# Loads of a decode layer spread over two DMA queues, in whole loads, with a smaller wq side load

## Chip, cores, metric

One core of one Trainium2 chip runs the whole program. The metric is the device time of one execution in microseconds (us), as the median of several executions; lower is better. "PE" is TensorE (PEld its weight loads), "DVE" is VectorE, "ACT" is ScalarE, "SP" is the engine that issues the DMAs of the sync queue. "SPq" and "ACTq" are DMA issues by those two.

## The reference, cut to what matters

One decoding step, batch 4, one token each: layer norm, attention with 32 query heads over the last 2048 positions of a cache with 4 KV heads, output projection, layer norm, SwiGLU. All tensors are bfloat16.

```python
q  = layernorm(x) @ wq                         # x 4x1024, wq 1024x4096
p  = softmax(q . k * 128**-0.5)                # k, v: 4 x 4 heads x 2048 x 128 are read
h  = x + (p @ v) @ wo                          # wo 4096x1024
hn = layernorm(h)
out = h + (silu(hn @ w1) * (hn @ w3)) @ w2     # w1, w3 1024x3584, w2 3584x1024
```

There are 55.6 MB to read and only four rows to work on, so the time is that of reading.

## The kernel before

All loads go through one 160 KiB wide ring of SBUF and one queue. A list gives their order; `load_next()` issues the next one at fixed places in the program. A load waits on SP until its place in the ring is free.

```python
def load_rows(at, src, n, r0, m):
    t = ring[:, at : at + m * n]
    nc.sync.dma_start(out=t, in_=src[:, r0 * n : (r0 + m) * n])
    ...
def load_kv(at, src, b):                 # two batches, two DMAs of 2 MB
    for k in range(BS): ... nc.sync.dma_start(...)

CE = 512
SETS = [(0, 5, 4), (80, 3, 2), (104, 3, 2)]      # first row, engines, column blocks
def load_side(r0, ne, ns): ...           # the last CE columns of the last wq row of 128
                                         # partitions, loaded into few partitions instead
def load_tail(at, src, n, r0, m): ...    # the second half of wq without those columns
plan = [
    ("wq", load_rows, (0, wq_v, N_Q, 0, 4)),
    ("side", load_side, SETS[0]), ("side", load_side, SETS[1]), ("side", load_side, SETS[2]),
    ("wq", load_tail, (32 * KIB, wq_v, N_Q, 4, 4)),
    ("k", load_kv, (64 * KIB, A_k_cache, 0)), ("k", load_kv, (96 * KIB, A_k_cache, 2)),
    ("v", load_kv, (128 * KIB, A_v_cache, 0)), ("v", load_kv, (0, A_v_cache, 2)),
    ("wo", load_rows, (32 * KIB, wo_v, D, 0, 32)),
    ("w1", load_rows, (96 * KIB, w1_v, N_F, 0, 8)),
    ("w3", ... two halves), ("w2", ... 17, 7, 3 and 1 rows),
]
```

The side loads are a tuned detail. A normal load uses 16 DMA engines, each with 8 of the 128 partitions. A side load uses only 5 or 3 of them. So 512 columns (1024 bytes) of one row of each partition are taken from all 16 engines (8 KB each) and given to five: 32 rows to three engines, 16 rows to two.

The K part transposes each tile on PE and copies it out of PSUM in turn on DVE and ACT:

```python
for u, (b, n) in enumerate(units):          # 16 units
    for t in range(NJ // TB):               # two tiles each
        ... 8 transposes on PE ...
        if nt % 2 == 0: nc.vector.tensor_copy(...)
        else:           nc.scalar.copy(...)
```

## Time and profile before

| | before |
|---|---|
| median (range) of runs at the time of the prediction | 138.0 us (137.88 to 138.04) |
| read from HBM | 55.59 MB |
| first byte to last landing | 1.7 to 132.8 us |
| rate in that stretch | 426 GB/s, DMA share 1.00 |
| last landing to end of the span | 3.4 us |

The first fence holds lines of the page of the kernel before: busy times by engine, then the span in 40 slices (busy share of the DMA engines in tenths, and GB/s), then the DMA queues with packets, MB and the share of the time of 16 engines.

```profile
PE 73.8 (54%) x1050; PEld 45.0 (33%) x1050; DVE 43.4 (32%) x79; ACT 31.1 (23%) x36; POOL 1.7 (1%) x8
...
DMA  5999999999999999999979999989899999989970
GB/s 156 463 464 404 404 438 405 424 428 438 433 428 419 429 443 428 429 522 477 462 327 443 481 409 404 477 371 477 354 430 426 438 455 442 430 389 419 421 288 5
...
q1 hardware_dynamic: 2731, 55.58, 95.6%
q8 instruction: 8, 0.13, 0.3%
q10 hardware_dynamic: 48, 0.02, 0.1%
q14 instruction: 2, 0.02, 0.0%
```

Queue q1 is the sync queue; it carries nearly everything (q10, ACT's, has 0.02 MB) and is never without work.

The next fence is the stretch table over 1.6 to 132.3 us (stretch and its length, busy time of PE, PEld, DVE, ACT, POOL with counts, PE clock, DMA share, GB/s).

```profile
1.60:132.30 130.70, 73.10 (x1039) 44.68 (x1043) 42.76 (x77) 30.72 (x35) 0.67 (x3) 0.79 1.00 426
```

A share of 1.00 says that the 16 engines were busy for the whole stretch. Then the timeline at the end (start us, busy us, engine, line, operation, in brackets the idle time before it and what ended it). `hgT` are the activations that w2 is multiplied with, `y_ps` the sum:

```profile
120.18 1.70 DVE L477 STREAM_TRANSPOSE hgT<-hg 128x896 bf16<-128x896 bf16 x1
...
126.09 3.82 PE L485 MATMUL y_ps<-ring,hgT 128*32 128x256 bf16 x68 [7.08 <-DMA ring<-in_B_w_dram]
...
130.34 1.22 PE L485 MATMUL y_ps<-ring,hgT 128*32 128x256 bf16 x28 [0.43 <-DMA ring<-in_B_w_dram]
...
132.18 0.92 PE L485 MATMUL y_ps<-ring,hgT 128*32 128x256 bf16 x16 [0.63 <-DMA ring<-in_B_w_dram]
...
133.15 0.37 ACT L495 CAST res<-y_ps 128x256 bf16<-128x256 f32 x1 [26.41 <-PE y_ps L485]
```

PE waits for w2's data at every step, so the end of the kernel is the last landing plus a fixed tail.

### The profile page before, as it was taken

Reading aid. Unit: us, or ns where it says so; the run is one execution under the profiler, and the core shown is the slowest. Engines: PE = TensorE matmul, PEld = TensorE weight load, DVE = VectorE, ACT = ScalarE, POOL = GpSimd, SP = SyncE. Lnnn points to the kernel's source line nnn. Section 1 sums busy time; section 2 is a strip of 40 time slices with the busy share of each in tenths; the row PEclk is TensorE's granted clock in tenths of the full one; section 3 lists DMA queues with packets and bytes.
Section 4 is the critical chain, followed back from the end, with each engine's and each line's share of the span. In section 5 each row is a group of like instructions: output and inputs, shape, how many; then the busy total and the mean of one; then the engine's idle time right before and its main releaser. Section 6 shows DMA issues by size and latency. Waiting matters only on the chain.

```text
span 136.1 us, 2343 instructions
## 1 busy us (share of the span) xinstructions
PE 73.8 (54%) x1050; PEld 45.0 (33%) x1050; DVE 43.4 (32%) x79; ACT 31.1 (23%) x36; POOL 1.7 (1%) x8
## 2 busy tenths in 40 slices
PE   0202980979898989810535906793096440900960
PEld 0200220267474747400024905571043210300840
DVE  6820000044243434471984001206100695080000
ACT  3000000016555555518385200000002300000001
POOL 5000000000000000000000000000000000000000
PEclk9999999999999999997555555579757777555577
DMA  5999999999999999999979999989899999989970
GB/s 156 463 464 404 404 438 405 424 428 438 433 428 419 429 443 428 429 522 477 462 327 443 481 409 404 477 371 477 354 430 426 438 455 442 430 389 419 421 288 5
DMA packets 2789, 55.75 MB, mean 410 GB/s; under 512 B 311, under 2 KB 471, under 8 KB 731
## 3 DMA queue, kind: packets, MB, share of 16 engines
q1 hardware_dynamic: 2731, 55.58, 95.6%
q8 instruction: 8, 0.13, 0.3%
q10 hardware_dynamic: 48, 0.02, 0.1%
q14 instruction: 2, 0.02, 0.0%
HBM read 55.59 MB, written 0.01 MB: 408 GB/s over the span
## 4 chain that ended last, share of the span: by engine, by line
DMA 54%; PE 24%; ACT 11%; DVE 5%; SPq 2%; issue 1%; ACTq 0%
DMA ring<-in_B_w_dram 40%; DMA ring<-in_A_wq_dram 15%; PE kt_ps L315 10%; ACT kT L321 5%; PE scores_ps L300 5%; ACT z L356 3%; PE q_ps L259 3%; SPq L119 2%; PE g_ps L455 2%; DVE rmax L332 2%; ACT Pm L337 2%; PE OT_ps L378 2%; DVE pT L346 1%; DVE z L352 1%; ACT L337 1%
## 5 line engine op out<-in xcount | busy, mean ns | idle before, releaser
L321 ACT COPY kT<-kt_ps 128x1024 bf16<-128x1024 bf16 x16 | 15.9, 1013 | 13.1 <-PE kt_ps L315 13.1
L315 PE MATMUL kt_ps<-ident,ring 128*128 128x128 bf16 x256 | 17.8, 230 | 0.0
L315 PEld LDWEIGHTS <-ring 128*128 128x128 bf16 x256 | 15.8, 104 | 4.9 <-issue 4.9
L319 DVE COPY kT<-kt_ps 128x1024 bf16<-128x1024 bf16 x16 | 11.1, 692 | 16.2 <-PE kt_ps L315 16.2
L259 PE MATMUL q_ps<-ring,xnT 128*4 128x512 bf16 x63 | 7.2, 626 | 10.5 <-DMA ring<-in_A_wq_dram 10.5
L378 PE MATMUL OT_ps<-z,ring 128*128 128x32 bf16 x256 | 7.5, 188 | 9.0 <-ACT z L356 5.0
L455 PEld LDWEIGHTS <-hnT 128*32 128x32 bf16 x128 | 5.3, 137 | 19.3 <-issue 16.6
L300 PE MATMUL scores_ps<-kT,qz 128*32 128x512 bf16 x64 | 9.9, 610 | 2.9 <-ACT kT L321 2.9
L455 PE MATMUL u_ps<-ring,hnT 128*32 128x448 bf16 x64 | 6.4, 576 | 8.2 <-DMA ring<-in_B_w_dram 8.2
L378 PEld LDWEIGHTS <-ring 128*128 128x128 bf16 x256 | 7.4, 105 | 9.8 <-issue 9.7
L485 PE MATMUL y_ps<-ring,hgT 128*32 128x256 bf16 x112 | 5.8, 375 | 8.3 <-DMA ring<-in_B_w_dram 8.1
L455 PE MATMUL g_ps<-ring,hnT 128*32 128x448 bf16 x64 | 5.5, 529 | 5.2 <-DMA ring<-in_B_w_dram 5.2
L485 PEld LDWEIGHTS <-hgT 128*32 128x32 bf16 x112 | 4.5, 130 | 10.2 <-issue 5.9
L259 PEld LDWEIGHTS <-xnT 128*4 128x4 bf16 x63 | 2.0, 115 | 14.8 <-issue 14.7
L277 DVE TENSOR_SCALAR q_sb<-q_ps 128x512 bf16<-128x512 f32 x1 | 0.7, 692 | 19.5 <-PE q_ps L259 19.5
L495 ACT CAST res<-y_ps 128x256 bf16<-128x256 f32 x1 | 0.4, 372 | 26.4 <-PE y_ps L485 26.4
L356 ACT ACTIVATE z<-pt_ps,mask 128x512 bf16<-128x512 f32 x8 | 5.3, 687 | 3.5 <-DVE z L352 3.5
L348 PE MATMUL pt_ps<-pT,perm 128*128 128x512 bf16 x4 | 2.4, 608 | 6.8 <-DVE pT L346 6.8
L278 ACT ACTIVATE q_sb<-q_ps 128x512 bf16<-128x512 f32 x1 | 0.6, 597 | 23.6 <-DVE q_sb L277 23.6
L405 PE MATMUL y_ps<-ring,o 128*32 128x256 bf16 x128 | 5.5, 352 | 0.8 <-DVE o L394 0.8
L352 DVE TENSOR_SCALAR z<-pt_ps,mask 128x512 bf16<-128x512 f32 x8 | 5.5, 738 | 1.2 <-ACT z L356 0.8
L469 DVE RECIPROCAL eg<-eg 128x896 f32<-128x896 f32 x1 | 5.8, 5754 | 0.0
(79 smaller groups left out, 50.2 us busy)
## 6 DMA issues: line engine op xcount, KB each, us to landing
ring<-in_A_k_cache_dram SPq DMA_DIRECT2D x4, 2048.0 KB, 25.4
ring<-in_A_v_cache_dram SPq DMA_DIRECT2D x4, 2048.0 KB, 39.0
ring<-in_B_w_dram SPq DMA_DIRECT2D x1, 7168.0 KB
ring<-in_B_w_dram SPq DMA_DIRECT2D x2, 3584.0 KB, 23.3
ring<-in_B_w_dram SPq DMA_DIRECT2D x1, 4352.0 KB
ring<-in_A_wq_dram SPq DMA_DIRECT2D x1, 4096.0 KB, 12.1
ring<-in_A_wq_dram SPq DMA_DIRECT2D x1, 3968.0 KB, 19.8
ring<-in_B_w_dram SPq DMA_DIRECT2D x1, 1792.0 KB
```

The costliest lines, as they stand in the source:

```text
L259: nc.tensor.matmul(q_ps[QD * g : QD * g + B, hf * 512 : hf * 512 + n], lhsT=xnT[:, kc, :], rhs=wq_t[:, c0 : c0 + n], start=(kc == 0), stop ...
L300: nc.tensor.matmul(scores_ps[QD * g : QD * (g + 1), n * 512 : (n + 1) * 512], lhsT=qz_v[:, z0 : z0 + QD], rhs=kT_v[:, g, :, :], start=(b = ...
L315: nc.tensor.transpose(out=kt_ps[:, jj, :], in_=k_v[:, n * NJ + t * TB + jj, :], identity=ident[:])
L319: nc.vector.tensor_copy(out=kT[:, t * TB : (t + 1) * TB, :], in_=kt_ps[:])
L321: nc.scalar.copy(out=kT[:, t * TB : (t + 1) * TB, :], in_=kt_ps[:])
L352: nc.vector.tensor_scalar(out=z[:, :, g, :], in0=pt_ps[:], scalar1=mask[:, g : g + 1], scalar2=None, op0=ALU.mult)
L356: nc.scalar.mul(out=z[:, :, g, :], in_=pt_ps[:], mul=mask[:, g : g + 1])
L378: nc.tensor.matmul(OT_ps[:, b, :], lhsT=loaded["v"][b][:, j, :], rhs=PTz[j // NJ][:, (j % NJ) * B + b, :, :], start=(j == 0), stop=(j == J ...
L405: nc.tensor.matmul(y_ps[QD * j : QD * (j + 1), :], lhsT=o4[:, i, :, :].rearrange("p b s -> p (b s)"), rhs=loaded["wo"][i][:, j * CG : (j + ...
L455: nc.tensor.matmul(out_ps[QD * j : QD * (j + 1), hf, :HF], lhsT=hnT[:, k, :], rhs=loaded[kind][k][:, c0 : c0 + HF], start=(k == 0), stop=( ...
L469: nc.vector.reciprocal(out=eg[:], in_=eg[:])
L485: nc.tensor.matmul(y2_ps[QD * j : QD * (j + 1), :], lhsT=hgT[:, i, :], rhs=loaded["w2"][i][:, j * CG : (j + 1) * CG], start=False, stop=(i ...
```

## The change

Its intent: spread whole loads over the sync queue and ACT's queue, so that two loads are in flight, and move fewer wq columns with fewer side loads. The number of bytes stays the same. The core of the diff:

```diff
-    BS = 2
-        nc.sync.dma_start(out=t, in_=...)                 # load_rows
+    def load_rows(at, src, n, r0, m, q=nc.sync):
+        tc.keep_in_program_order(q.dma_start(out=t, in_=...))
+    def load_kv(at, src, b, q=nc.sync):                   # one batch, one DMA
-    CE = 512
-    SETS = [(0, 5, 4), (80, 3, 2), (104, 3, 2)]
+    CE = 352
+    SETS = [(0, 5, 4), (80, 3, 4)]
+    Q2 = nc.scalar
         ("k", load_kv, (96 * KIB, A_k_cache, 2)),
+        ("k", load_kv, (112 * KIB, A_k_cache, 3, Q2)),
         ("v", load_kv, (128 * KIB, A_v_cache, 0)),
+        ("v", load_kv, (144 * KIB, A_v_cache, 1, Q2)),
         ("v", load_kv, (0, A_v_cache, 2)),
+        ("v", load_kv, (16 * KIB, A_v_cache, 3, Q2)),
-        ("w1", load_rows, (96 * KIB, w1_v, N_F, 0, 8)),
+        ("w1", load_rows, (96 * KIB, w1_v, N_F, 0, 4)),
+        ("w1", load_rows, (124 * KIB, w1_v, N_F, 4, 4, Q2)),
-        ("w3", load_rows, (28 * KIB, w3_v, N_F, 4, 4)),
+        ("w3", load_rows, (28 * KIB, w3_v, N_F, 4, 4, Q2)),
...
+        load_next({1: 2, 4: 2, 7: 2}.get(u, 0))           # in the K loop
```

More of the change, by code (lines that the diff above doesn't have):

```diff
@@ L88 @@
     ring = stream.tile([P, RING], BF16)
-    def load_rows(at, src, n, r0, m):
+    def load_rows(at, src, n, r0, m, q=nc.sync):
         t = ring[:, at : at + m * n]
-        nc.sync.dma_start(out=t, in_=src[:, r0 * n : (r0 + m) * n])
+        tc.keep_in_program_order(q.dma_start(out=t, in_=src[:, r0 * n : (r0 + m) * n]))
         return [t[:, k * n : (k + 1) * n] for k in range(m)]
-    def load_kv(at, src, b):
-        out = []
-        for k in range(BS):
-            v = ring[:, at + k * JK * Dh : at + (k + 1) * JK * Dh]
-            nc.sync.dma_start(
-                out=v,
-                in_=src[b + k, :, Sk - W : Sk, :].rearrange("g (pp j) d -> pp g (j d)", pp=PK),
-            )
-            out.append(v.rearrange("p (j d) -> p j d", d=Dh))
-        return out
+    def load_kv(at, src, b, q=nc.sync):
+        v = ring[:, at : at + JK * Dh]
+        rows = src[b, :, Sk - W : Sk, :].rearrange("g (pp j) d -> pp g (j d)", pp=PK)
+        tc.keep_in_program_order(q.dma_start(out=v, in_=rows))
+        return [v.rearrange("p (j d) -> p j d", d=Dh)]
     N_Q, N_F = Hq * Dh, F
-    CE = 512
-    SETS = [(0, 5, 4), (80, 3, 2), (104, 3, 2)]
+    CE = 352
+    SETS = [(0, 5, 4), (80, 3, 4)]
     def load_side(r0, ne, ns):
@@ L131 @@
         ("side", load_side, SETS[1]),
-        ("side", load_side, SETS[2]),
         ("wq", load_tail, (32 * KIB, wq_v, N_Q, 4, 4)),
         ("k", load_kv, (64 * KIB, A_k_cache, 0)),
+        ("k", load_kv, (80 * KIB, A_k_cache, 1)),
         ("k", load_kv, (96 * KIB, A_k_cache, 2)),
+        ("k", load_kv, (112 * KIB, A_k_cache, 3, Q2)),
         ("v", load_kv, (128 * KIB, A_v_cache, 0)),
+        ("v", load_kv, (144 * KIB, A_v_cache, 1, Q2)),
         ("v", load_kv, (0, A_v_cache, 2)),
+        ("v", load_kv, (16 * KIB, A_v_cache, 3, Q2)),
         ("wo", load_rows, (32 * KIB, wo_v, D, 0, 32)),
-        ("w1", load_rows, (96 * KIB, w1_v, N_F, 0, 8)),
+        ("w1", load_rows, (96 * KIB, w1_v, N_F, 0, 4)),
+        ("w1", load_rows, (124 * KIB, w1_v, N_F, 4, 4, Q2)),
         ("w3", load_rows, (0, w3_v, N_F, 0, 4)),
-        ("w3", load_rows, (28 * KIB, w3_v, N_F, 4, 4)),
+        ("w3", load_rows, (28 * KIB, w3_v, N_F, 4, 4, Q2)),
         ("w2", load_rows, (56 * KIB, w2_v, D, 0, 17)),
@@ L158 @@
     nc.scalar.dma_start(out=x_sb[:], in_=x_flat)
-    load_next(8)
+    load_next(7)
     ident = const.tile([P, P], BF16)
@@ L263 @@
                     start=(kc == 0),
-                    stop=(kc == KC - 1 or (kc == KC - 2 and c0 + 512 == N_Q)),
+                    stop=(kc == KC - 1),
+                    skip_group_check=(c0 + 512 == N_Q),
                 )
         if kc == RQ - 1:
-            load_next()
             for k, np_ in enumerate(sl):
@@ L274 @@
                     stop=False,
+                    skip_group_check=True,
                 )
@@ L325 @@
             emit_scores(u - 1)
-        if u == NSB * BS - 1:
-            load_next()
+        load_next({1: 2, 4: 2, 7: 2}.get(u, 0))
     emit_scores(len(units) - 1)
+    load_next()
     rmax = act.tile([P, 1], FP32)
@@ L384 @@
             )
-        if b % BS == BS - 1:
+        if b % 2 == 1:
             load_next()
```

## The prediction

> **What bounds the kernel now.** The 16 DMA engines. The DMA view gives 55.6 MB read. The stretch table over 1.6 to 132.3 us shows a DMA share of 1.00 and 426 GB/s. The Trainium skill, page "DMA: Bandwidth & Descriptors", section Specifications, names a fabric ceiling of 435 GB/s; the trace agrees (packets of 28 to 64 KB move at 27.0 to 27.1 GB/s per engine, 16 KB packets at 26.8). So there is no idle time to fill: what is idle is 1.7 us before the first byte and 3.4 us after the last load (matmuls, cast, store). PE is busy 54%. By the chain of waits PE ends last because w2 lands last, at 132.8 us.
>
> The records of packets and landings show engine skew: per load, 11 engines land about 1.5 us before the slowest after wq; at the end 5 are early (131.0 to 131.6 us) and 11 late (132.4 to 132.8). Eight instruction fetches of 16 KB each cost one engine about 1.4 us (0.94 for the fetch, 0.5 more for the packet it overlaps). Side loads cost their engines a comparable amount; the late group is both kinds together.
>
> **What the change does.**
> 1. Two queues. The same skill page ("Issuing engines are not separate DMA queues") says both run on the same 16 engines and interleave. Bytes stay the same, and the single queue never ran dry: w1 was issued at 76.0 us, wo landed at 80.1 to 82.1. Only the few ns per packet can shrink. Estimate: K/V loads follow each other in 4.83 to 4.90 us against 4.82 at the ceiling; over the whole kernel at most 0.5 us.
> 2. Order. From K batch 3 on two loads share the engines, so each lands later. k2 lands near 43 us instead of 38.2, when its transposes start. w1's first half may land near 101 instead of 98.9, w3's first half near 116 with its second half earlier. Then 64 instead of 32 w3 matmuls (2 x 3.2 us) follow 116 us: hgT is ready near 125.3 instead of 121.9, still before w2 lands (126.1). Slack falls from 4.1 to under 1 us.
> 3. ACT issues five loads, about 0.6 us each (its issues now: 0.58 to 0.66). The three in the K phase may lengthen it by 0.5 to 2 us; loads are queued ahead of it.
> 4. CE 352. Each engine that carries no side load moves 2.5 KB more: 0.1 us later at the end. One side issue fewer (0.87 us on SP) and shorter side matmuls are hidden behind wq's loads.
>
> **On the critical path:** up to -0.5 us (packets), +0.1 us (balance), 0 to +0.5 us (w2 starting late, more delayed instruction fetches).
>
> **Predicted:** 137.8 us, 137.0 to 138.8 in 8 of 10. Faster by over 2%: 0.03; within 2%: 0.94; slower: 0.03.
>
> **Signs.** Right: bytes unchanged, 426 to 429 GB/s from first byte to last, last landing within 1 us of 132.8, a second queue carrying about 13 to 14 MB, w1 and w3 halves landing close together, K phase ending later without a later finish. Wrong step 2: PE idle before w2's first matmul ended by DVE, not DMA.
>
> **What would make it wrong.** Two active queues raising or lowering an engine's rate; instruction fetches waiting behind two large packets and stalling PE at the tail; fetches falling on other engines, so that the last engine ends more than 0.5 us earlier or later; ACT blocked by a load's wait while a copy is due.

## The result

The changed kernel took 138.48 us in the median of four runs (138.25 to 138.55), the kernel before 138.02 us (137.88 to 138.08). The ratio is 1.0032, with a 95% interval from 1.0014 to 1.0049. A ratio here is the mean time of one kernel's fast runs over that of the other's of the same rounds, so not quite the ratio of the medians. The change costs 0.3%: small, within 2% as forecast, but clear of noise and of the opposite sign to the forecast 137.8.

The same lines of the page of the changed kernel:

```profile
PE 73.1 (53%) x1051; PEld 45.0 (33%) x1051; DVE 43.1 (32%) x77; ACT 31.4 (23%) x36; POOL 1.7 (1%) x8
...
DMA  5999999999999999999999989999999999999960
GB/s 156 461 462 424 404 394 433 432 417 441 436 417 441 408 441 436 499 405 465 403 489 432 408 362 453 433 428 410 428 445 436 424 420 432 479 408 388 413 251 2
...
q1 hardware_dynamic: 2152, 41.94, 71.9%
q10 hardware_dynamic: 768, 13.66, 23.4%
q8 instruction: 8, 0.13, 0.3%
q14 instruction: 2, 0.02, 0.0%
```

ACT's queue (q10) now carries 13.66 MB, a quarter. The stretch table of the changed kernel:

```profile
1.60:132.30 130.70, 72.25 (x1035) 44.64 (x1036) 42.54 (x75) 31.01 (x35) 0.67 (x3) 0.78 1.00 426
```

The share and the rate are what they were. Two queues neither filled anything nor slowed the 16 engines together. The end of the timeline of the changed kernel:

```profile
122.89 1.70 DVE L476 STREAM_TRANSPOSE hgT<-hg 128x896 bf16<-128x896 bf16 x1
...
126.59 3.82 PE L484 MATMUL y_ps<-ring,hgT 128*32 128x256 bf16 x68 [4.88 <-DMA ring<-in_B_w_dram]
...
130.84 1.01 PE L484 MATMUL y_ps<-ring,hgT 128*32 128x256 bf16 x28 [0.42 <-DMA ring<-in_B_w_dram]
...
132.65 0.94 PE L484 MATMUL y_ps<-ring,hgT 128*32 128x256 bf16 x16 [0.81 <-DMA ring<-in_B_w_dram]
...
133.64 0.37 ACT L494 CAST res<-y_ps 128x256 bf16<-128x256 f32 x1 [24.06 <-PE y_ps L484]
```

The activations are ready 2.7 us later than before (the transpose starts at 122.89, not 120.18), yet PE's wait still ends with the DMA. So the reordered loads ate slack only. What moved is the moment at which each part of w2 is complete and PE goes on: 126.59 instead of 126.09, 130.84 instead of 130.34, and the cast at the end 133.64 instead of 133.15. These are the 0.5 us of the two profiled runs (138.55 and 138.01).

### Which engine was last

In these traces a load over all 16 engines leaves 16 landing records, one for each engine, and PE goes on after the last of them. Here are the 16 landing times of the last w2 load, sorted, from the trace's landing records:

```
before: 130.97 131.09 131.30 131.64 132.40 132.41 132.41 132.45 132.58 132.59 132.61 132.62 132.68 132.69 132.76 132.77
after:  131.03 131.21 131.35 131.56 132.43 132.44 132.51 132.64 132.65 132.66 132.76 132.78 132.79 132.87 132.91 133.26
```

Fifteen engines are about where they were, at most 0.19 us later. One is 0.35 us behind all the others, and the kernel waits for it. (The prediction speaks of 5 early engines and 11 late ones; for this load the list of the kernel before has 4 and 12.)

The packet records have no engine number. But an engine starts each packet 3 to 4 ns before the recorded end of the packet before it, and all the engines go through the same known list of loads. With these two rules the records fall into 16 chains. The bytes of each chain confirm the split: each engine without side rows has 3.468 MB in the changed kernel, plus 16 KB exactly where a fetch of q8 is in its chain. This is a reconstruction of mine. Its table, one line per engine (end of its last w2 packet, side rows that it carries, instruction fetches on it):

```
before                                    after
130.68   0 rows                           130.69   0 rows
130.73   0 rows                           130.92   0 rows
131.01   0 rows                           131.06   0 rows
131.32  16 rows                           131.25  16 rows
132.07   0 rows  16 KB at  86.1           132.11  32 rows
132.10   0 rows  16 KB at 104.1           132.16  32 rows
132.13  32 rows                           132.18   0 rows  16 KB at  86.2
132.13   0 rows  16 KB at  42.9           132.22   0 rows  16 KB at 130.9
132.27   0 rows  16 KB at  92.6           132.29   0 rows  16 KB at  93.7
132.30  32 rows                           132.34   0 rows  16 KB at 106.5
132.31   0 rows  16 KB at  54.6           132.35  16 rows   8 KB at  60.6
132.32   0 rows  16 KB at  31.5           132.49   0 rows  16 KB at  54.1
132.34   0 rows  16 KB at 130.4           132.50   0 rows  16 KB at  80.1
132.37  32 rows                           132.52   0 rows  16 KB at  42.0
132.41   0 rows  16 KB at  80.1           132.61   0 rows  16 KB at  27.5
132.46  16 rows   8 KB at  60.2           132.93  32 rows   8 KB at  93.9
```

The kernel before is in balance. Eight engines are hit by a 16 KB fetch, each by one, and each is held up by 1.40 to 1.42 us: about 0.9 us for the fetch and 0.5 us more for the packet that follows (after the fetch at 130.4, spread over the next four packets, which are of 2 KB). None of the eight has side rows. The engines with 32 rows end together with them, and so does the one with 16 rows and an 8 KB fetch (0.84 us). The changed kernel has an 8 KB fetch that the kernel before hasn't: at 93.9 us, on an engine with 32 rows, 0.78 us. That engine is the last one.

The DMA view of 65 to 134 us shows the extra packet. Kernel before:

```profile
q1 hardware_dynamic: 1120, 28.31, 95.4%
q8 instruction: 5, 0.08, 0.4%
```

Changed kernel:

```profile
q1 hardware_dynamic: 963, 20.12, 67.8%
q10 hardware_dynamic: 362, 8.29, 28.1%
q8 instruction: 5, 0.08, 0.4%
q14 instruction: 1, 0.01, 0.0%
```

Both pages count two q14 packets. In the kernel before they come at 60.2 and 135.6 us, the second after the last load; in the changed kernel at 60.6 and 93.9 us.

Whose instructions are they? In all the traces with such a second packet, it starts when ACT has begun 63 to 69 of the instructions that the trace has (64 in the kernel before at 135.6 us, 64 in the changed kernel at 93.9 us). The first q14 packet, at 55.3 to 60.6 us in all twelve traces, does not follow ACT: ACT has then begun anything from 21 to 57 instructions, DVE 59 to 67. Where ten copies move from ACT to DVE (e6 and e10 below) it comes at 56.3 and 55.3 us instead of 60.6; where copies are added to ACT (e7, e8) it stays near 60, at 59.0 and 60.5. The q8 packets go with PE: in the kernel before the first four come after 241, 505, 771 and 1217 of its instructions (weight loads counted), and the fourth comes after 1217 in eleven of the twelve kernels, whose ACT streams run from 53 to 90 instructions in the trace. Their spacing is not even, though. So the second q14 packet is read here as an instruction fetch of ACT, the first as one of DVE, and q8 as PE's. The Trainium skill agrees in part: "Runtime: NRT & Kernel Launch", section Terms, says that the engines' instruction memory is refilled in 16 KiB blocks (the q8 packets are 16 KB, these two q14 packets 8 KB), and "CRC Debugging", section Comparing the Two Runs, puts the sequencers' refill DMAs on queue 14 (here on q8 too).

So the theory (A): the five loads on ACT's queue are five more instructions, with their waits eight more, in ACT's stream. ACT reaches its next block before the last load instead of after it, the fetch goes through one of the 16 busy engines, and it meets one of the three that carry most side rows. The smaller CE adds a little on all the engines without side rows.

Rivals: (B) two queues at once cost every engine something; (D) the smaller CE is the cause, as the balance is off. A fourth, that w2 waits for the activations, falls with the timeline above.

### The profile page after: what moved, and what is told of

Its sections match the earlier page's. It is cut to its first block, busy times and chain, and to the rows that moved or that the text cites. A ratio compares the mean times of both kernels' runs of the same rounds, so it can differ in the third digit from the quotient of the medians.

```text
span 136.7 us, 2344 instructions
## 1 busy us (share of the span) xinstructions
PE 73.1 (53%) x1051; PEld 45.0 (33%) x1051; DVE 43.1 (32%) x77; ACT 31.4 (23%) x36; POOL 1.7 (1%) x8
## 3 DMA queue, kind: packets, MB, share of 16 engines
q10 hardware_dynamic: 768, 13.66, 23.4%
HBM read 55.59 MB, written 0.01 MB: 407 GB/s over the span
## 4 chain that ended last, share of the span: by engine, by line
DMA 82%; PE 12%; SPq 2%; ACT 1%; DVE 1%; issue 0%; ACTq 0%
DMA ring<-in_B_w_dram 56%; DMA ring<-in_A_wq_dram 15%; DMA ring<-in_A_k_cache_dram 11%; PE kt_ps L315 5%; PE q_ps L258 3%; PE g_ps L454 2%; PE scores_ps L300 2%; SPq L113 1%; PE qt_ps L281 1%; ACT kT L321 1%; DVE q_sb L277 1%; SPq L92 0%; ACT res L494 0%; PE y_ps L484 0%; ACTq L321 0%
## 5 line engine op out<-in xcount | busy, mean ns | idle before, releaser
L315 PE MATMUL kt_ps<-ident,ring 128*128 128x128 bf16 x256 | 19.1, 230 | 1.2 <-DVE kT L319 0.7
L454 PE MATMUL u_ps<-ring,hnT 128*32 128x448 bf16 x64 | 5.4, 519 | 9.1 <-DMA ring<-in_B_w_dram 9.1
L454 PE MATMUL g_ps<-ring,hnT 128*32 128x448 bf16 x64 | 6.1, 577 | 7.2 <-DMA ring<-in_B_w_dram 7.2
```

The lines of the kernel that those rows point to most:

```text
L315: nc.tensor.transpose(out=kt_ps[:, jj, :], in_=k_v[:, n * NJ + t * TB + jj, :], identity=ident[:])
L454: nc.tensor.matmul(out_ps[QD * j : QD * (j + 1), hf, :HF], lhsT=hnT[:, k, :], rhs=loaded[kind][k][:, c0 : c0 + HF], start=(k == 0), stop=( ...
```

## The experiments

Ten kernels, five rounds each; all gave correct results. "Cost" is what the second q14 packet (ACT's fetch) delayed its engine in the profiled run, from the reconstruction; the next columns give the end of the latest engine and the time of the same run.

| run | median us | ratio to before (95%) | ACT fetch (2nd q14) at, on rows | cost us | latest engine | profiled run us |
|---|---|---|---|---|---|---|
| before | 138.02 | | 135.6, after the loads | | 132.46 | 138.01 |
| after | 138.48 | 1.0032 (1.0014 to 1.0049) | 93.9, 32 rows | 0.78 | 132.93 | 138.55 |
| e1_queues_only | 138.61 | 1.0049 (1.0036 to 1.0061) | 94.0, 32 rows | 0.67 | 132.89 | 138.50 |
| e2_cols_only | 138.04 | 1.0005 (0.9992 to 1.0018) | 136.0, after the loads | | 132.68 | 138.18 |
| e3_one_queue | 138.00 | 0.9998 (0.9984 to 1.0011) | 135.9, after the loads | | 132.49 | 138.01 |
| e4_w_on_act | 138.08 | 1.0006 (0.9993 to 1.0018) | 111.9, 32 rows | 0.55 | 132.66 | 138.22 |
| e5_kv_on_act | 138.39 | 1.0028 (1.0015 to 1.0041) | 104.5, 32 rows | 0.66 | 132.85 | 138.37 |
| e6_two_queues_no_fetch | 138.13 | 1.0011 (0.9999 to 1.0023) | none | | 132.57 | 138.15 |
| e7_one_queue_fetch | 138.12 | 1.0013 (1.0001 to 1.0025) | 71.6, 32 rows | 0.55 | 132.76 | 138.28 |
| e8_fetch_earlier | 138.09 | 1.0009 (0.9996 to 1.0022) | 71.3, 32 rows | 0.55 | 132.58 | 138.12 |
| e9_even_side | 138.36 | 1.0031 (1.0018 to 1.0043) | 93.6, 28 rows | 0.62 | 132.93 | 138.53 |
| e10_queues_no_fetch | 138.20 | 1.0014 (1.0001 to 1.0028) | none | | 132.53 | 138.20 |

In all twelve profiled runs the time less the end of the latest engine is 5.50 to 5.67 us. The latest engine decides the time.

### Taking the change apart

**e1_queues_only**: the changed kernel with the side loads as before (cut: a third side load in the list and the lines that go with it).

```diff
-    CE = 352
-    SETS = [(0, 5, 4), (80, 3, 4)]
+    CE = 512
+    SETS = [(0, 5, 4), (80, 3, 2), (104, 3, 2)]
```

> The changed kernel with 512 wq columns moved in three side loads, as before; the queues and the order stay changed. Before 138.0, after 138.5 us. Theory A (the last of 16 engines sets the end; the 0.5 us is 0.1 us of extra wq bytes on the engines without side loads plus 0.35 us of one straggler engine that is hit by one more instruction fetch, the 8 KB one near 94 us): 138.3 to 138.4, the last landing near 133.1 us, one landing some 0.35 us behind the others. Theory B (switching between two queues costs every engine): 138.4 to 138.5, all engines later by about the same. Theory D (the wq share alone is the cause): 138.0.

It came out at 138.61, worse than the changed kernel. (D) falls: without the smaller CE the loss is not less. In the profiled run the engine with 32 rows and the fetch at 94.0 us ends at 132.89, next after it 132.45. The expectation of 138.3 to 138.4 missed: it took 0.1 us off for CE, though a larger CE gives the loaded engines more, and the straggler is one of those.

**e2_cols_only**: the kernel before with `CE = 352` and two side loads.

> The kernel before with 352 wq columns moved in two side loads, one queue as before. Theory A: 138.1 us, plus 0.1 us on the unsided engines, last landing near 132.9, no straggler, no 8 KB instruction fetch near 94 us. Theory B: 138.0. Theory D: 138.4 to 138.5.

138.04: the columns alone cost nothing that can be told from zero. The 0.1 us that was expected lies inside the interval.

**e3_one_queue**: the changed kernel with `Q2 = nc.sync`.

> The changed kernel with every load on the sync queue: same loads, same sizes, same 352 columns. Theory A: 138.1 us, since ACT has five instructions' worth of issues fewer and its fetch near 94 us goes away; last landing near 132.9, no straggler. Theory B: 138.0 to 138.1. Theory D: 138.5.

138.00: cutting the loads differently, another order and CE 352 cost nothing on one queue. So the loss needs ACT's issues. (A) and (B) are still both possible.

**e4_w_on_act** and **e5_kv_on_act** split ACT's five loads. In e4 `Q2` is taken from K batch 3 and V 1, 3; in e5 from the halves of w1 and w3.

> The changed kernel with only the two weight halves (w1, w3) on ScalarE's queue; K batch 3 and V 1, 3 go to the sync queue. Theory A: what counts is where the 8 KB instruction fetch of ACT falls; with two issues instead of five it should come later than 94 us or after the last load, then 138.1 us, otherwise a straggler and 138.4 to 138.5. Theory B: two queues are active for 36 of the some 65 us that they were, so about half the loss: 138.25.

> The changed kernel with only K batch 3 and V 1, 3 on ScalarE's queue; the halves of w1 and w3 go to the sync queue. Counting the instructions of ACT in the traces so far, its second 8 KB instruction fetch comes with its 64th instruction; here that falls between 94 and 112 us. Theory A (one more fetch in front of the last load, on an engine that is already late): between 138.1 and 138.5, with an engine some 0.3 us behind the rest in the last landing if it is over 138.3. Theory B (two queues at once cost every engine, in the K and V stage): 138.4 to 138.5.

e4 lost nothing clear (1.0006), e5 nearly all (1.0028). Under (A) alone that is a surprise for e4, as its fetch comes before the last load and on an engine with 32 rows. The reconstruction shows the size: 0.55 us in e4, 0.66 in e5. From 0.55 us the straggler of e4 is 0.20 us behind the next engine in the profiled run, which was its slowest run (138.22; the others 138.00 to 138.16). Under (B) e4 and e5 should have shared the loss, unless only the K and V stage costs, as (B) is put for e5: 138.39 is at the edge of what it asked for there. These two runs do not decide that; e6, e8 and e10 do.

### Taking the fetch away, or adding it

**e6_two_queues_no_fetch**: the changed kernel, with ten ACT copies less. DVE has time for them.

```diff
-            if nt % 2 == 0:
+            if nt % 2 == 0 or u >= 6:
                 nc.vector.tensor_copy(...)
```

> The changed kernel whole, both queues as in it, but the K copies of units 6 to 15 all go to VectorE, so that ScalarE has 10 instructions fewer and its 64th comes after the last load. Theory A: no 8 KB instruction fetch between 65 and 133 us, no straggler, last landing near 132.9, 138.0 to 138.15 us. Theory B: 138.4 to 138.5, as the queues are used alike.

138.13, where (B) asked for 138.4 to 138.5. The DMA view of 65 to 134 us of this kernel has no q14 line, with the queues used as in the changed kernel:

```profile
q1 hardware_dynamic: 968, 20.45, 68.9%
q10 hardware_dynamic: 331, 7.78, 26.3%
q8 instruction: 5, 0.08, 0.4%
```

No engine with side rows stands behind the rest: the three with 32 rows end by 132.11, the latest of all, with a fetch of PE, at 132.57.

**e10_queues_no_fetch**: the same edit on e1, the worst kernel.

> The queues-only kernel (512 columns in three side loads as before, 138.61) with the K copies of units 6 to 15 on VectorE, so that ACT's 64th instruction and its fetch come after the last load. Account: two queues cost nothing by themselves, so as before, 137.9 to 138.1. Rival (the two queues themselves): 138.5 to 138.65.

138.20 instead of 138.61, so most of the loss is gone with the fetch; but it isn't quite the 137.9 to 138.1 that was expected. Some 0.1% (0.01 to 0.28) is left. The edit also moves copies to DVE, so neither run isolates the fetch perfectly. The intervals of e1 (from 1.0036) and e10 (to 1.0028) do not meet; those of the changed kernel and e6 overlap a little, but no run of e6 (137.98 to 138.19) is as slow as the fastest of the changed kernel (138.25).

**e7_one_queue_fetch**: the kernel before, with ten one-element copies on ACT before the q phase.

```diff
+    dum = const.tile([P, 16], FP32)
+    for i in range(10):
+        nc.scalar.copy(out=dum[:1, i : i + 1], in_=eps_t[:1, :])
```

> The kernel before with 10 one-element copies on ScalarE in its idle time before the q phase, so that its 64th instruction comes near 94 us; one queue. Theory A: 138.2 to 138.4, with one engine some 0.3 us behind in the last landing (138.0 to 138.1 if the fetch meets an early engine). Theory B: 138.0, as one queue is used.

138.12, ratio 1.0013, just clear of 1. The fetch came at 71.6 us, not near 94. It met an engine with 32 rows, which ended at 132.76, 0.28 us behind the next. So the straggler can be made on one queue, with no change to a load. Its cost of 0.55 us is the small one again, and so is the loss. (B) expected 138.0.

**e8_fetch_earlier**: the changed kernel, with 14 such copies, so that the fetch moves.

> The changed kernel with 14 such copies, so that the fetch moves some 20 to 30 us earlier. Theory A: as the engines have no idle time, a fetch costs the same whenever it comes before the last load: 138.2 to 138.6, unless it meets an early engine. Theory B: 138.5.

138.09. This misses (A) as it was put: the fetch at 71.3 us is on an engine with 32 rows, and yet the time is nearly that of the kernel before. The reconstruction shows a cost of 0.55 us instead of 0.78; that engine ends at 132.48, below the latest at 132.58. (B) falls here: both queues are used as in the changed kernel, and most of the loss is gone (all five runs, 138.00 to 138.17, are below the changed kernel's fastest, though the intervals overlap a little).

So a fetch doesn't cost the same whenever it comes. At 71 us and at 112 us it cost 0.55 us, between 93 and 105 us 0.62 to 0.78. With an engine that is otherwise level with the rest, this is the difference between 0.1% and 0.3 to 0.5%. Why the cost differs isn't settled. In the changed kernel, e5 and e9 a 16 KB fetch of PE was in flight at the same time or had ended less than 0.3 us before it; in e1 it had ended 0.6 us earlier; in the three cheap ones the nearest was over 4 us away. That is a coincidence in seven runs, not a test, and it does not carry over to the first q14 packet: that one cost 0.83 to 0.84 us in all twelve runs, in nine of them with the nearest fetch of PE over 4 us away.

### Moving the side rows

**e9_even_side**: the changed kernel, the same columns spread evenly (cut as in e1).

```diff
-    SETS = [(0, 5, 4), (80, 3, 4)]
+    SETS = [(0, 5, 4), (80, 5, 2), (120, 2, 1)]
```

> The changed kernel with the same 352 columns spread evenly: 24 rows on each of five engines (four more on two of them) instead of 32 on three and 16 on two. ACT's fetch near 94 us has landed on a fully loaded engine in every trace, the one near 60 us on a half loaded one. Account (sum of side rows and fetches on one engine): the engine with the second fetch carries 4 to 8 rows fewer, so it ends 0.15 to 0.3 us earlier, the one with the first fetch as much later; 138.2 to 138.35 against 138.48 of the changed kernel. Rival (the two queues themselves, or the fetch wherever it falls): 138.4 to 138.6.

138.36, no gain, but the engines did as the account says. The one with the second fetch and now 28 rows ended at 132.46 instead of 132.93, among the rest. The one with the first q14 fetch (60.6 us; the expectation takes it for ACT's) rose from 16 to 24 rows and from 132.35 to 132.93, and was now the straggler, 0.41 us behind the next. The forecast for the total was 138.2 to 138.35: the first fetch (0.83 us) is the dearer of the two, and that was not weighed. It suggests why the tuned side loads are uneven: with the uneven ones, the first q14 fetch is on an engine with the lesser side load in every trace.

No version beat the kernel before. There is little left to win: three engines without rows and fetches end some 1.5 us early, but the side loads cannot reach them, as all the side rows went to the same five engines.

## Why the prediction was right or wrong

- **Class, range: right.** 138.48 lies within 137.0 to 138.8, and "within 2%" held. The core of the argument held too: 55.59 MB, DMA share 1.00 and 426 GB/s in both kernels. It agrees with the Trainium skill, "DMA: Bandwidth & Descriptors", section Issuing engines are not separate DMA queues, by which loads of different issuers share the same 16 engines.
- **Sign: wrong.** The sum was given as 137.8, 0.2 us less than before; it was 0.5 us more. The range held because bytes and rate held; its centre counted on a gain that did not come.
- **Step 1, "at most 0.5 us" less from packets: nothing came.** The rate stayed 426 GB/s, and e3 (one queue) at 138.00 is no slower than the kernels with two.
- **Step 2, order: nearly right.** w1's first half landed at 101.08 us (forecast 101), w3's last part at 116.28 (116), hgT was ready at 124.6 (125.3), before w2 (126.55). k2 landed at 39.7, not near 43. PE's wait for w2 was ended by the DMA, so of "0 to +0.5 us (w2 starting late, more delayed instruction fetches)" the first part was 0. The second part names the right kind of cost, without saying which fetch or why.
- **Step 3, the K phase "0.5 to 2 us" longer: wrong.** It ended at 57.96 us instead of 58.27. The timeline of ACT in the changed kernel shows why an issue held up nothing:

```profile
32.35 1.01 ACT L321 COPY kT<-kt_ps 128x1024 bf16<-128x1024 bf16 x1 [0.55 <-PE kt_ps L315]
32.36 0.61 ACTq L99 DMA_DIRECT2D ring<-in_A_k_cache_dram  x1
33.90 1.01 ACT L321 COPY kT<-kt_ps 128x1024 bf16<-128x1024 bf16 x1 [0.54 <-PE kt_ps L315]
```

  The issue of 0.61 us runs while ACT copies, and the next copy waits for PE.
- **Step 4, CE 352, "0.1 us later": not shown.** e2 has 1.0005 (0.9992 to 1.0018).
- **The step that failed is the list of costs of an ACT issue.** It counted the issue time, 0.6 us, which cost nothing, and not the place in ACT's instruction stream. "Eight instruction fetches of 16 KB each cost one engine about 1.4 us" was right (1.40 to 1.42 us measured), but the prediction left out the 8 KB fetches, of which the changed kernel has one more before the last load, 0.78 us on an engine that was level with the latest. Without it the loss was 0.35 us less (e6 against the changed kernel) and 0.41 us less (e10 against e1). Among the things that would make it wrong it had named "fetches falling on other engines". That is close to what happened, though here a further fetch came rather than the old ones moving.
- **How much is settled.** With the fetch out of the way, two queues cost 0.11% (-0.01 to 0.23, e6) and 0.14% (0.01 to 0.28, e10) against the kernel before; with it 0.32% and 0.49%. The rest, some 0.1%, is open, and so is what sets the cost of one fetch.

## What to carry to other kernels

When the 16 DMA engines are busy throughout, as here (share 1.00), the time is that of the latest engine (in twelve runs it ended 5.50 to 5.67 us before the measured time): look at the spread of the 16 landings of the last load, not at the mean rate. The instruction fetches seen here ran on these DMA engines and delayed the loads (0.55 to 0.84 us for 8 KB), so even an instruction on an idle engine can cost something if it brings a fetch in before the last load. A second queue did not help this stream, which never ran dry, and the tuned balance of bytes between DMA engines held only for the instruction stream that it was tuned with.

## What the Trainium skill lacked or had wrong

- "DMA: Bandwidth & Descriptors", section Queues, rings and completion order, names the refills as traffic of an internal row, but no page gives a figure for their cost to a load stream: a 16 KB fetch held up one engine by 1.40 to 1.50 us (less where it came among an engine's last packets), an 8 KB one by 0.55 to 0.84 us.
- No page says which DMA engine serves a fetch. In all twelve traces PE's fetches fell on different engines, none with side rows, and the 8 KB fetches on q14 on engines with side rows.
- "Runtime: NRT & Kernel Launch", section Terms: refills in 16 KiB blocks. The q8 packets are of 16 KB; the two on q14, which go with the counts of DVE and ACT, are of 8 KB.
- "CRC Debugging", section Comparing the Two Runs: refills on queue 14. Here those that follow PE's count are on q8.
- "DMA: Bandwidth & Descriptors", section Specifications: about 358 GB/s as the limit from HBM for one core. This case, with one core running, read 426 GB/s over 130.7 us, near the 435 GB/s that the same section gives for the fabric: for such a case the HBM row of that table is too low.
